# Retention and two MLPs on one core: scores of eight heads at once in block 1's chunks, key halves of heads 4 to 7 exchanged from chunk 0, block 1's norm by four small matmuls

## The chip, the cores and the metric

The kernel runs on one core of one Trainium2 chip. The core has TensorE (PE, with its weight loads listed as PEld), VectorE (DVE), ScalarE (ACT), GpSimd (POOL) and SyncE (SP), which here issues most DMAs. The metric is the device time of one launch in microseconds; lower is better.

## The reference

Three layers over 4 x 768 = 3072 tokens of 512 features, all in float32:

```
for t in range(S):                                   # retention, 8 heads of 64, state 64 x 64 per head
    state = gamma[h] * state + k[t] (outer) v[t]
    y[t]  = scale * q[t] @ state
x  = y as [3072, 512]
xn = x / sqrt(mean(x*x, -1) + 1e-6) * rms_g          # RMS norm
x  = (silu(xn @ w_gate) * (xn @ w_val)) @ w_out      # 512 -> 1536 -> 512
h  = x @ w_in                                        # 512 -> 1024
e  = exp(h - max(h));  solu = h * e / (sum(e) + 1e-9)
out = (solu - mean) / sqrt(var + 1e-6) * g_ln @ w_out2   # 1024 -> 512
```

## The kernel before, in words

The 3072 tokens are 6 blocks of 512, a block is 4 chunks of 128 tokens, and 6 chunks make one of the 4 batches. Retention is computed chunk by chunk: scores of keys against queries inside the chunk (a matmul), times a table of decays `mtab` that is zero above the diagonal (the mask, on DVE), times the values; to that the state `U` of the chunks before adds its part through `qd` (queries times `qtab`), and `kd` (keys times `ktab`) makes the state's update. `kd` and `qd` are products on POOL.

All large matmuls are done in three, as high and low halves of both operands (`mm3`, lines 719 to 721; each 128 x 128 weights and 512 columns). For block n the loop `bc_block` goes over 12 groups of the hidden features: gate into PSUM bank GB, value into VB, Silu on ACT (L764), product on DVE (L736), split into halves on ACT and DVE (L98, L99), and `cmm` sums the output into X0 to X3. `de_block` is the last MLP. Block 5 goes through `seven_block`, with 7 instead of 8 products per pair.

Weights come as packed 64-bit words. While block 0 runs, each of the 36 tiles of 512 KB is loaded (L595, a ring of four buffers `x`), turned into float32 (ACT L617, DVE L619, POOL L620; the sign on ACT into PSUM bank YB, L625; DVE L632 joins them), split into halves (ACT L98, DVE or POOL L99) and used; ACT's queue stores the halves to DRAM (`scr`) for later blocks. From the end of block 0 on the 16 tiles of the last MLP follow the same way (`w2i`, `w2o`).

Retention and norm of block n+1 are cut into pieces and laid in slots of block n (`extra`, `att_pieces`). Block 0's own chunks 0 to 3 stand at the start (`first_*`). A list scheduler with its own timeline then decides the order of the instructions on each engine; `run` (L117 issues its matmuls) keeps a group of matmuls together, and `issue_after` pins one instruction behind another.

There are two ways of doing a chunk before:

- Chunks 4 to 7 (block 1, while block 0 runs) go by units of 4 heads: `unit_load` (L137, L140, L143), `unit_prep` (L153, L161), `unit_scores` (L169: 4 matmuls of 64 rows x 128 keys x 128 queries into bank SB; mask L171) and `unit_out`.
- Chunks 8 to 23 go by all 8 heads: `att_load` (8 loads of 64 rows, L215, and 3 for keys and values), `att_prep` (L232, L237), `att_scores` (16 matmuls of 64 x 64 tiles of the array, a 64-key half each, without the half above the diagonal, into SB and YB; 6 masks L258, 4 memsets L260). Keys of heads 4 to 7 lie with their halves exchanged there, so `turn_tables` loads those halves of `mtab` and `ktab` the other way round between chunk 7 and chunk 8.

Block 1's norm has a path of its own: `rms_1` (four one-column matmuls L328, then L329 and L330 make `rinv`, the inverse root, one column per chunk), `rms_2` (L334: DVE lays `rinv` on a diagonal, 128 x 512; L337: one float32 matmul with ones spreads it over the partitions, into SB), `rms_mul` (four products L340), `xn_split` (halves `xnh`, `xnl`).

Of the kernel before, what the change touches and what calls it, by code (L numbers as in the profile page):

```python
# [9 lines left out]
F32 = mybir.dt.float32  # L10
# [30 lines left out]
def retention_moe_kernel(ctx: ExitStack, tc: tile.TileContext, qk0, q2, kt, kv, wpk, w2i, w2o,  # L41
# [92 lines left out]
    def unit_load(gc, u):  # L134
        gap("gq", 416)
        tq = wt("rq", [P, 4, P], F32, 2)
        nc.sync.dma_start(tq, q2[gc, u])  # L137
        if u == 0:
            rawk[gc] = wt("rk", [P, 4, P], F32, 2)
            nc.sync.dma_start(rawk[gc], kt[gc])  # L140
        gap("gr", 96)
        tv = wt("rv", [P, 512], F32, 2)
        nc.sync.dma_start(tv, kv[gc, u])  # L143
        raw[gc, u] = (tq, tv)

    def unit_prep(gc, u):
        tq, tv = raw.pop((gc, u))
        tk = rawk[gc] if u == 0 else rawk.pop(gc)
        kd = qd = None
        if gc % CPB != CPB - 1:  # L150
            gap("gd", 416)
            kd = wt("kd", [P, 4, 64], F32, 2)
            nc.gpsimd.tensor_tensor(  # L153
                out=kd, in0=tv[:, 0:256].rearrange("p (h d) -> p h d", h=4),
                in1=ktab_t[:, 4 * u:4 * u + 4].unsqueeze(2).to_broadcast([P, 4, 64]), op=ALU.mult)
        if gc % CPB != 0:
            qd = wt("qd", [P, 2, P], F32, 2)
            tq4 = tq.rearrange("p (a b) i -> p a b i", b=2)
            for hh in range(2):
                r = halfrows(hh)  # L160
                nc.gpsimd.tensor_tensor(out=qd[r], in0=tq4[r, :, hh, :],  # L161
                                        in1=qtab_t[r, 2 * u:2 * u + 2, :], op=ALU.mult)
        r = halfrows(u)
        prepd[gc, u] = (tk[r], tq[r], tv, kd, qd)

    def unit_scores(gc, u):
        tk, tq, tv, kd, qd = prepd[gc, u]
        for hl in range(4):
            nc.tensor.matmul(SB[:, hl * P:hl * P + P], lhsT=tk[:, hl, :], rhs=tq[:, hl, :], start=True, stop=True)  # L169
        A = masked[gc, u] = wt("r2", [P, 4, P], F32, 8)  # L170
        nc.vector.tensor_tensor(out=A, in0=SB.rearrange("p (h i) -> p h i", h=4),  # L171
                                in1=mtab_t[:, 4 * u:4 * u + 4, :], op=ALU.mult)

    def unit_out(gc, u):

        tk, tq, tv, kd, qd = prepd.pop((gc, u))
        A = masked.pop((gc, u))
        first, last = gc % CPB == 0, gc % CPB == CPB - 1
        ps = slice(2 * u, 2 * u + 2)
        calls = []  # L180
        if not first:
            calls += [mm(SB[:, pl * P:pl * P + P], U[gc % 2][:, 2 * u + pl, :], qd[:, pl, :], pl == 0, False)
                      for pl in range(2)]
        for pl in range(2):
            for hh in range(2):
                hl = 2 * pl + hh
                calls.append(mm(SB[halfrows(hh), pl * P:pl * P + P], tv[:, 256 + 64 * hl:320 + 64 * hl],
                                A[:, hl, :], first, first or pl == 1))
        sv = SB[:, 256:384].rearrange("p (a e) -> p a e", a=2)
        if not last:  # L190
            for pl in range(2):
                for hh in range(2):
                    hl = 2 * pl + hh
                    calls.append(mm(sv[halfrows(hh), pl, :], kd[:, hl, :], tv[:, 256 + 64 * hl:320 + 64 * hl],
                                    True, True))
        run(calls)
        if not last:
            for hh in range(2):
                decay_add(gc, halfrows(hh), ps, sv[halfrows(hh)])
        c = gc % NCB  # L200
        cs = slice(c * P, c * P + P)
        nc.scalar.copy(xT[:, ps, cs], SB[:, 0:256].rearrange("p (a i) -> p a i", a=2))
        if u:
            sq = f4()[:, 0, :].rearrange("p (a i) -> p a i", a=4)
            nc.scalar.activation(sq, xT[:, :, cs], AF.Square)
            nc.vector.tensor_reduce(out=ssq[:, cs], in_=sq.rearrange("p a i -> p i a"), axis=AX.X, op=ALU.add)

    def att_load(gc):
        tq, tk = wt("rq", [P, 4, P], F32, 2), wt("rk", [P, 4, P], F32, 2)
        tv = wt("rv", [P, 2, 512], F32, 2)  # L210
# [5 lines left out]
        nc.sync.dma_start(tv[:, 0], kv[gc, 0])  # L216
        for r in range(2):
            nc.sync.dma_start(tv[halfrows(r), 1], kv[gc, 1, halfrows(1 - r)])
        raw[gc] = (tq, tk, tv)

    def turn_tables():

        for r in range(2):
            nc.sync.dma_start(mtab_t[halfrows(r), 4:8, :], mtab[halfrows(1 - r), 4:8, :])
            nc.sync.dma_start(ktab_t[halfrows(r), 4:8], ktab[halfrows(1 - r), 4:8])

    def att_prep(gc):
        tq, tk, tv = raw.pop(gc)
        kd = qd = None
        if gc % CPB != CPB - 1:  # L230
            kd = wt("kd", [P, 2, 4, 64], F32, 2)
# [99 lines left out]

    def rms_2(bank):

        nc.vector.tensor_tensor(out=ssq.rearrange("p (c i) -> p c i", c=NCB),  # L334
                                in0=ident.unsqueeze(1).to_broadcast([P, NCB, P]),
                                in1=rinv.unsqueeze(2).to_broadcast([P, NCB, P]), op=ALU.mult)
        nc.tensor.matmul(bank, lhsT=ones, rhs=ssq, start=True, stop=True)  # L337

    def rms_mul(bank, k):
        nc.vector.scalar_tensor_tensor(out=xT[:, k, :], in0=xT[:, k, :], scalar=rg_t[:, k:k + 1], in1=bank,  # L340
# [159 lines left out]
    def att_pieces(n):  # L500

        out = []
        if n == 1:
            units = [(gc, u) for gc in range(NCB, 2 * NCB) for u in range(2)]
            ahead = units + [(2 * NCB,), (2 * NCB + 1,)]
            for i, (gc, u) in enumerate(units):
                nxt, nx2 = ahead[i + 1], ahead[i + 2]

                def a(gc=gc, u=u, nxt=nxt):
                    unit_scores(gc, u)  # L510
                    if len(nxt) == 1:
                        turn_tables()

                def b(nxt=nxt):
                    (unit_prep if len(nxt) == 2 else att_prep)(*nxt)

                def c(gc=gc, u=u, nx2=nx2):
                    unit_out(gc, u)
                    (unit_load if len(nx2) == 2 else att_load)(*nx2)

                out += [a, b, c]
# [321 lines left out]
    def seven_2(j, part, y, q):  # L843
# [5 lines left out]
        room[2] += 1  # L849
        V = nc.vector  # L850
        V.tensor_tensor(out=y[:, 0, hi], in0=d, in1=q[:, lo], op=ALU.add)
        V.tensor_tensor(out=y[:, 1, lo], in0=c, in1=q[:, lo], op=ALU.add)

    def seven_block(n):
        base = n * NM
        for j in range(NM // 2):
# [19 lines left out]
            nc.scalar.activation(gf[:, 256:], gf[:, 256:], AF.Silu)  # L876
            if j and not final:
                out(m - 1)
            seven_2(j, 1, *v)
# [1 line left out]
            nc.vector.tensor_tensor(out=vf[:, lo], in0=quads[1][0], in1=gf[:, lo], op=ALU.mult)  # L881
            nc.vector.tensor_tensor(out=vf[:, hi], in0=vf[:, hi], in1=gf[:, hi], op=ALU.mult)
            if final and PRE & 2:
                nc.scalar.activation(wt("sm", [P, 12], F32, 4)[:, 0:1], gf[:, 0:1], AF.Exp)
            for i in range(2):
                if i:
                    nc.vector.tensor_tensor(out=vf[:, 512:], in0=vf[:, 512:], in1=gf[:, 512:], op=ALU.mult)
# [352 lines left out]
```

## Time and profile before

| | |
|---|---|
| median of 3 runs | 993.0 us (991.95 to 993.1) |
| profiled execution | 992.89 us, its span 991.1 us, so 1.8 us lie around the span |
| mean granted TensorE clock | 0.995 |
| PE busy | 975.8 us of the span |
| DVE, ACT, POOL busy | 466.0, 398.0, 422.9 us |
| DMA | 211.90 MB, 214 GB/s on average |

A busy share over the whole span is an average of stages: chunks 0 to 3 (about 35 us), block 0 with its weight conversions (to about 159 us), and the rest. In a row of the timeline, "x8" joins eight records of one kind; the profile writes two records for each float32 matmul of the scores. "[1.50 <-ACT xT L202]" means that the engine stood idle for 1.50 us until the named instruction ended.

### The profile page before, as it was taken

The page shows a single profiled execution, that of the slowest core. Times are in us where ns is not written, and L with a number is a line of the kernel's source. Part 1 is how long each engine was busy: PE and PEld are TensorE (multiplying, and loading weights), DVE is VectorE, ACT ScalarE, POOL GpSimd, SP SyncE. Part 2 cuts the span into 40 slices and gives each one's busy share as a digit, 9 for nine tenths or more (in the row PEclk, how much of TensorE's full clock was granted, in tenths as well). Part 3 has the DMA queues.
Part 4 walks back from the last instruction along what each step waited for, and adds up shares of the span by engine and source line. Part 5 has one row for each costly group of instructions (what it writes and reads, how often), then busy time and mean ns, then how long its engine had stood idle before and what let it go on. Part 6 is the DMA issues. An engine that isn't in the chain of part 4 may idle for free.

```text
span 991.1 us, 15941 instructions
## 1 busy us (share of the span) xinstructions
PE 975.8 (98%) x5910; PEld 811.3 (82%) x5910; DVE 466.0 (47%) x921; ACT 398.0 (40%) x770; POOL 422.9 (43%) x517
## 2 busy tenths in 40 slices
PE   8899999999999999999999999999999999999998
PEld 8778787787888887888888888788888888999887
DVE  5788784563364743234462224462323353443552
ACT  4767664573344443222443122344212344221433
POOL 6876873672142593243644223644042382000031
PEclk9899999999999999999999999999999999999999
DMA  9699999796612135799522889622597724697200
GB/s 353 230 327 406 356 309 382 275 340 214 213 38 76 54 105 188 278 301 302 187 75 97 287 284 304 221 71 100 170 347 268 264 84 149 205 308 263 75 12 32
DMA packets 91021, 211.90 MB, mean 214 GB/s; under 512 B 10432, under 2 KB 36416, under 8 KB 90944
## 3 DMA queue, kind: packets, MB, share of 16 engines
q1 hardware_dynamic: 82160, 185.71, 55.3%
q10 hardware_dynamic: 8784, 25.17, 6.5%
q8 instruction: 47, 0.77, 0.3%
q14 instruction: 30, 0.25, 0.1%
HBM read 172.05 MB, written 38.80 MB: 213 GB/s over the span
## 4 chain that ended last, share of the span: by engine, by line
PE 86%; POOL 4%; DVE 3%; DMA 2%; ACT 2%; issue 2%; SPq 0%; ACTq 0%; POOLq 0%; DVEq 0%
PE X L719 12%; PE X L720 11%; PE X L721 11%; PE GB L719 7%; PE GB L721 7%; PE GB L720 6%; PE VB L719 6%; PE VB L720 6%; PE VB L721 6%; PE SB L117 3%; PE YB L117 2%; PE VB L825 2%; PE YB L825 2%; POOL st L620 1%; PE SB L825 1%
## 5 line engine op out<-in xcount | busy, mean ns | idle before, releaser
L736 DVE TENSOR_TENSOR f<-VB,f 128x512 f32<-128x512 f32 x60 | 41.3, 689 | 159.2 <-PE VB L721 151.4
L719 PE MATMUL X<-r,wo 128*128 128x512 f32 x264 | 101.7, 396 | 2.1 <-ACT r L98 1.5
L720 PE MATMUL X<-r,wo 128*128 128x512 f32 x264 | 103.4, 392 | 0.0
L721 PE MATMUL X<-r,wo 128*128 128x512 f32 x264 | 103.0, 390 | 0.0
L764 ACT ACTIVATE f<-GB 128x512 f32<-128x512 f32 x60 | 35.6, 594 | 147.6 <-PE GB L721 145.3
L98 ACT CAST r<-f 128x512 fp32r<-128x512 f32 x72 | 44.5, 619 | 120.8 <-DVE f L736 101.3
L620 POOL TENSOR_TENSOR st<-st,x 128x512 int32<-128x512 int32 x52 | 71.4, 1377 | 50.4 <-ACT st L994 11.6
L719 PE MATMUL GB<-xnh,w 128*128 128x512 f32 (+1 forms) x220 | 86.7, 394 | 2.7 <-ACT xnh L98 1.3
L719 PE MATMUL VB<-xnh,w 128*128 128x512 f32 (+1 forms) x220 | 85.8, 390 | 0.0
L720 PE MATMUL GB<-xnl,w 128*128 128x512 f32 (+1 forms) x220 | 85.6, 389 | 0.1
L721 PE MATMUL VB<-xnh,w 128*128 128x512 f32 (+1 forms) x220 | 85.2, 387 | 0.3 <-POOL w L99 0.3
L721 PE MATMUL GB<-xnh,w 128*128 128x512 f32 (+1 forms) x220 | 85.5, 388 | 0.0
L720 PE MATMUL VB<-xnl,w 128*128 128x512 f32 (+1 forms) x220 | 85.2, 387 | 0.0
L99 DVE TENSOR_TENSOR r<-f,r 128x512 fp32r<-128x512 f32 x72 | 61.9, 861 | 30.7 <-ACT r L98 30.2
L560 POOL TENSOR_TENSOR x<-x 128x512 f32<-128x512 f32 x24 | 30.8, 1288 | 105.2 <-DMA x<-scr 83.1
L950 POOL TENSOR_TENSOR sm<-sm 128x1 f32<-128x1 f32 x24 | 5.3, 222 | 138.3 <-DVE sm L928 121.0
L719 PEld LDWEIGHTS X<-r,wo 128*128 128x128 f32 x264 | 49.4, 188 | 13.3 <-ACT r L98 2.1
L721 PEld LDWEIGHTS X<-r,wo 128*128 128x128 f32 x264 | 49.6, 188 | 10.3
L720 PEld LDWEIGHTS X<-r,wo 128*128 128x128 f32 x264 | 49.6, 188 | 10.2 <-DVE r L99 0.2
L719 PE MATMUL X<-w2oh,r 128*128 128x512 f32 (+1 forms) x144 | 56.6, 393 | 0.0
L721 PE MATMUL X<-w2oh,r 128*128 128x512 f32 (+1 forms) x144 | 55.7, 387 | 0.0
L720 PE MATMUL X<-w2ol,r 128*128 128x512 f32 (+1 forms) x144 | 55.3, 384 | 0.0
(370 smaller groups left out, 2420.1 us busy)
## 6 DMA issues: line engine op xcount, KB each, us to landing
w<-scr SPq DMA_DIRECT2D x96, 512.0 KB, 4.6
wo<-scr SPq DMA_DIRECT2D x60, 512.0 KB, 4.4
x<-in_wpk SPq DMA_DIRECT2D x36, 512.0 KB, 6.6
x<-scr SPq DMA_DIRECT2D x24, 512.0 KB, 6.7
sscr<-x SPq DMA_DIRECT2D x24, 512.0 KB, 7.7
scr<-CV ACTq DMA_DIRECT2D x18, 512.0 KB, 6.5
rv<-in_kv SPq DMA_DIRECT2D x24, 256.0 KB, 4.6
scr<-w ACTq DMA_DIRECT2D x12, 512.0 KB, 6.0
```

What stands on the lines that cost most here:

```text
L98: h = nc.scalar.copy(hi, src)
L99: (lo_eng or nc.vector).tensor_tensor(out=lo, in0=src, in1=hi.bitcast(F32), op=ALU.subtract)
L117: return lambda: nc.tensor.matmul(out, lhsT=lhsT, rhs=rhs, start=start, stop=stop)
L560: nc.gpsimd.tensor_tensor(out=w[:, 0, :], in0=w[:, 0, :], in1=w[:, 1, :], op=ALU.add)
L620: nc.gpsimd.tensor_tensor(out=ti, in0=ti, in1=lo, op=ALU.add)
L719: nc.tensor.matmul(ps, lhsT=lh, rhs=rh, start=start, stop=False)
L720: nc.tensor.matmul(ps, lhsT=lh, rhs=rl, start=False, stop=False)
L721: nc.tensor.matmul(ps, lhsT=ll, rhs=rh, start=False, stop=stop)
L736: recent["dve"] = nc.vector.tensor_tensor(out=a, in0=GV[1], in1=silu[:, 0, :], op=ALU.mult)
L764: recent["act"] = nc.scalar.activation(s[:, 0, :], GV[0], AF.Silu)
L825: nc.tensor.matmul(ps, lhsT=x, rhs=y[:, k, :], start=start and k + i == 0, stop=k == 1 and i == 2, skip_group_check=True)
L950: G.tensor_tensor(out=w, in0=r, in1=r, op=ALU.mult)
```

## The change

Chunks 4 to 7 use `att_load`, `att_prep` and `att_scores`, as chunks 8 to 23 do, and a new `half_out` for the output of four heads at a time. The score banks are SB and YB, so YB alternates between the masks and the signs of the weight conversion. The key halves of heads 4 to 7 are exchanged from chunk 0: the tables are loaded so at the start, `kv_load` replaces one load by three in chunks 0 to 3, `first_scores` becomes 16 matmuls per chunk, and `turn_tables` is gone. Block 1's `rms_2` becomes four matmuls that take a broadcast column of `rinv` as weights and the identity as data, with no work on DVE. In block 5 one sum for the second half moves behind the first half's products, and the load of the Exp table is pinned behind the last Silu.

```
-    def unit_scores(gc, u):
-        tk, tq, tv, kd, qd = prepd[gc, u]
-        for hl in range(4):
-            nc.tensor.matmul(SB[:, hl * P:hl * P + P], lhsT=tk[:, hl, :], rhs=tq[:, hl, :], start=True, stop=True)
-        A = masked[gc, u] = wt("r2", [P, 4, P], F32, 8)
-        nc.vector.tensor_tensor(out=A, in0=SB.rearrange("p (h i) -> p h i", h=4),
-                                in1=mtab_t[:, 4 * u:4 * u + 4, :], op=ALU.mult)
...
+    def half_out(gc, u):
+        tq, tk, tv, kd, qd = prepd[gc] if u == 0 else prepd.pop(gc)
+        A = [masked[gc, hh] if u == 0 else masked.pop((gc, hh)) for hh in range(2)]
...
+    def kv_load(t, gc):
+        nc.sync.dma_start(t[:, 0], kv[gc, 0])
+        for r in range(2):
+            nc.sync.dma_start(t[halfrows(r), 1], kv[gc, 1, halfrows(1 - r)])
...
     def rms_2(bank):
-        nc.vector.tensor_tensor(out=ssq.rearrange("p (c i) -> p c i", c=NCB),
-                                in0=ident.unsqueeze(1).to_broadcast([P, NCB, P]),
-                                in1=rinv.unsqueeze(2).to_broadcast([P, NCB, P]), op=ALU.mult)
-        nc.tensor.matmul(bank, lhsT=ones, rhs=ssq, start=True, stop=True)
+        for c in range(NCB):
+            nc.tensor.matmul(bank[:, c * P:c * P + P], lhsT=rinv[:, c:c + 1].to_broadcast([P, P]), rhs=ident,
+                             start=True, stop=True)
...
     def first_load(c):
         nc.sync.dma_start(QK[:, c], qk0[c])
-        nc.sync.dma_start(KV[:, c], kv[c].rearrange("u p x -> p u x"))
+        kv_load(KV[:, c], c)
     def first_scores(c, banks):
-        run([mm(banks[hh][:, p * P:p * P + P], QK[halfrows(hh), c, 1, p, :], QK[halfrows(hh), c, 0, p, :], True, True)
-             for p in range(4) for hh in range(2)])
+        run([mm(banks[hh][halfrows(half), p * P:p * P + P],
+                QK[halfrows(hh), c, 1, p, halfrows(half if p < 2 else 1 - half)], QK[halfrows(hh), c, 0, p, :], True, True)
+             for p in range(4) for hh, half in ((0, 0), (1, 1), (0, 1), (1, 0))])
...
+            for gc in range(NCB, 2 * NCB):
+                out += [lambda gc=gc: att_scores(gc), lambda gc=gc: att_prep(gc + 1), lambda gc=gc: half_out(gc, 0),
+                        lambda gc=gc: (half_out(gc, 1), att_load(gc + 2))]
...
     def seven_2(j, part, y, q):
...
-        V.tensor_tensor(out=y[:, 1, lo], in0=c, in1=q[:, lo], op=ALU.add)
+        if part == 0:
+            V.tensor_tensor(out=y[:, 1, lo], in0=c, in1=q[:, lo], op=ALU.add)
...
     nc.sync.dma_start(QK[:, 0], qk0[0])
-    nc.sync.dma_start(mtab_t, mtab)
-    nc.sync.dma_start(ktab_t, ktab)
+    for t, src in ((mtab_t, mtab), (ktab_t, ktab)):
+        nc.sync.dma_start(t[:, 0:4], src[:, 0:4])
+        for r in range(2):
+            nc.sync.dma_start(t[halfrows(r), 4:8], src[halfrows(1 - r), 4:8])
     nc.sync.dma_start(utab_t, utab)
-    nc.sync.dma_start(KV[:, 0], kv[0].rearrange("u p x -> p u x"))
+    kv_load(KV[:, 0], 0)
...
-    unit_load(NCB, 0)
-    unit_load(NCB, 1)
-    unit_prep(NCB, 0)
+    att_load(NCB)
+    att_load(NCB + 1)
+    att_prep(NCB)
```

What this does to the order on TensorE, at the scores of one chunk among the matmuls of block 0. Before, one unit of four heads (lines 719 to 721 are the large matmuls, `CV` and `w` weights):

```order
216 L719 MATMUL GB<-xnh,CV 128x512
217 L720 MATMUL GB<-xnl,CV 128x512
218 L169 MATMUL SB<-rq_630,rk_632 128x128 x4
219 L721 MATMUL GB<-xnh,CV 128x512
220 L719 MATMUL GB<-xnh,CV 128x512
```

And of the changed kernel the group of eight heads (left out are three more pairs of each shape), whose large matmuls are lines 666 to 668:

```order
307 L668 MATMUL GB<-xnh,w_85_845 128x512
308 L117 MATMUL YB<-rq_567,rk_568 64x128
309 L117 MATMUL SB<-rq_567,rk_568 64x128
...
316 L117 MATMUL YB<-rq_567,rk_568 64x64
317 L117 MATMUL SB<-rq_567,rk_568 64x64
...
324 L666 MATMUL GB<-xnh,w_85_845 128x512
325 L667 MATMUL GB<-xnl,w_85_845 128x512
```

Two groups of four full-width matmuls per chunk have become one group of sixteen, eight of 64x128 and eight of 64x64, in turns into YB and SB.

The second place is TensorE at the end of block 0, around the matmul that spreads `rinv`. Before (`xnh` with `CV` is still block 0's last value group, with `w_202` it is block 1's first gate):

```order
554 L720 MATMUL VB<-xnl,CV 128x512
555 L337 MATMUL SB<-ssq,ones 128x512
556 L721 MATMUL VB<-xnh,CV 128x512
557 L719 MATMUL VB<-xnh,CV 128x512
558 L720 MATMUL VB<-xnl,CV 128x512
559 L721 MATMUL VB<-xnh,CV 128x512
560 L721 MATMUL X_70<-r_200_1575,wo_1425 128x512
561 L720 MATMUL X_71<-r_201_1576,wo_1425 128x512
562 L721 MATMUL X_71<-r_200_1575,wo_1425 128x512
563 L719 MATMUL GB<-xnh,w_202_1593 128x512
```

And now (`w_188` is block 1's first gate tile):

```order
676 L668 MATMUL X_69<-r_192_1739,CV 128x512
677 L667 MATMUL X_70<-r_193_1740,CV 128x512
678 L668 MATMUL X_70<-r_192_1739,CV 128x512
679 L667 MATMUL X_71<-r_193_1740,CV 128x512
680 L668 MATMUL X_71<-r_192_1739,CV 128x512
681 L297 MATMUL SB<-ident,rinv 128x128 x4
682 L666 MATMUL GB<-xnh,w_188_1698 128x512
683 L666 MATMUL VB<-xnh,w_190_1718 128x512
```

Seven matmuls of block 0 stood between the spreading matmul and block 1's first; now none does, and all of block 0's stand ahead of it.

The third place is SP's queue of loads at the start. Before, to the third-last of the rows that the chunks' loads and the first weight tiles share:

```order
19 L595 DMA x_31_438<-in_wpk 128x512
20 L137 DMA rq_508<-in_q 128x512
21 L140 DMA rk_510<-in_kt 128x512
22 L143 DMA rv_513<-in_kv 128x512
23 L137 DMA rq_515<-in_q 128x512
24 L143 DMA rv_517<-in_kv 128x512
25 L140 DMA rk_632<-in_kt 128x512
26 L595 DMA x_34_450<-in_wpk 128x512
27 L595 DMA x_37_462<-in_wpk 128x512
28 L595 DMA x_40_474<-in_wpk 128x512
```

And now (L184 are the loads of 64 rows):

```order
26 L184 DMA rk_553<-in_kt 64x2x128 x4
27 L184 DMA rq_552<-in_q 64x2x128
28 L542 DMA x_34_494<-in_wpk 128x512
29 L184 DMA rq_552<-in_q 64x2x128 x3
30 L171 DMA rv_555<-in_kv 128x512
31 L173 DMA rv_555<-in_kv 64x512
32 L542 DMA x_37_506<-in_wpk 128x512
33 L173 DMA rv_555<-in_kv 64x512
34 L184 DMA rk_568<-in_kt 64x2x128 x3
35 L542 DMA x_40_518<-in_wpk 128x512
```

The weight tile `x_40` had 27 loads ahead of it (each row's "x" counted); now it has 47, nearly all of the new ones of 64 rows.

## Rows read from the trace of the kernel before

**Rows 1.** The page: busy time of TensorE; the chain that ended last.

```profile
PE 975.8 (98%) x5910; PEld 811.3 (82%) x5910; DVE 466.0 (47%) x921; ACT 398.0 (40%) x770; POOL 422.9 (43%) x517
...
PE 86%; POOL 4%; DVE 3%; DMA 2%; ACT 2%; issue 2%; SPq 0%; ACTq 0%; POOLq 0%; DVEq 0%
```

**Rows 2.** Waits of TensorE: line, releaser, us in total, times, longest.

```profile
PE X L719 <- ACT r L98: 1.5, 1, 1.5
PE SB L169 <- ACT xT L202: 1.5, 1, 1.5
...
PE GB L719 <- ACT xnh L98: 1.3, 1, 1.3
...
PE VB L721 <- POOL w L99: 0.3, 1, 0.3
```

**Rows 3.** Timeline of TensorE around one unit's scores: start, us, operation.

```profile
80.12 0.39 PE L720 MATMUL VB<-xnl,w 128*128 128x512 f32 x1
80.44 1.16 PE L169 MATMUL SB<-rq,rk 64*128 64x128 f32 x8
...
81.87 0.39 PE L719 MATMUL VB<-xnh,w 128*128 128x512 f32 x1
```

**Rows 4.** The same around the eight heads' scores of a later chunk.

```profile
265.76 0.39 PE L719 MATMUL X<-r,wo 128*128 128x512 f32 x1
...
266.22 0.39 PE L721 MATMUL X<-r,wo 128*128 128x512 f32 x1
266.54 0.32 PE L117 MATMUL YB<-rq,rk 64*64 64x128 f32 x1
...
267.70 0.39 PE L720 MATMUL GB<-w2il,x 128*128 128x512 f32 x1
```

**Rows 5.** Masks on DVE, by line: count, ns min/median/max, first and last.

```profile
L171 DVE TENSOR_TENSOR r<-SB,mtab_t x8: 678/686/693, 39.3 to 135.0; 128x512 f32<-128x512 f32 x8
...
L258 DVE TENSOR_TENSOR A<-YB,mtab_t x48: 270/294/426, 243.6 to 765.1; 64x128 f32<-64x128 f32 x32, 128x256 f32<-128x256 f32 x16
```

**Rows 6.** The products kd and qd on POOL, by line.

```profile
L153 POOL TENSOR_TENSOR kd<-rv,ktab_t x6: 612/1001/1069, 35.0 to 126.6; 128x256 f32<-128x256 f32 x6
...
L161 POOL TENSOR_TENSOR qd<-rq,qtab_t x12: 719/734/1175, 35.6 to 119.6; 64x256 f32<-64x256 f32 x12
...
L232 POOL TENSOR_TENSOR kd<-rv,ktab_t x13: 1033/1045/1489, 140.9 to 651.2; 128x512 f32<-128x512 f32 x13
...
L237 POOL TENSOR_TENSOR qd<-rq,qtab_t x14: 1272/1287/1722, 133.6 to 691.0; 128x512 f32<-128x512 f32 x14
```

**Rows 7.** The chain that ended last, at the start and at 39 us.

```profile
2.58 0.43 SPq L1042
3.06 5.87 DMA QK<-in_qk
...
38.95 0.69 POOL qd L161
```

**Rows 8.** Timeline of all engines where block 1 begins.

```profile
154.72 1.02 PE L337 MATMUL SB<-ssq,ones 128*128 128x512 f32 x2
...
155.78 2.72 DVE L340 SCALAR_TENSOR_TENSOR xT<-xT,rg_t,SB 128x512 f32<-128x512 f32 x4 [4.21 <-PE SB L337]
...
157.99 2.18 ACT L98 CAST xnh<-xT 128x512 fp32r<-128x512 f32 x4 [3.50 <-DVE xT L340]
...
158.66 0.49 PE L719 MATMUL GB<-xnh,w 128*128 128x512 f32 x1 [1.29 <-ACT xnh L98]
```

**Rows 9.** Windows of 25 us: busy us per engine, clock, DMA share, GB/s.

```profile
25.00:50.00 25.00, 22.24 (x153) 19.62 (x153) 19.02 (x30) 17.98 (x34) 22.60 (x25) 0.86 0.68 231
...
75.00:100.00 25.00, 25.00 (x123) 20.04 (x121) 20.47 (x29) 17.68 (x32) 16.89 (x15) 1.00 1.03 411
```

**Rows 10.** Waits of ACT up to 180 us, for the weight tiles' loads.

```profile
ACT x L617 <- DMA x<-in_wpk: 5.7, 5, 1.8
```

**Rows 11.** SP's issues of 64-row loads of a later chunk.

```profile
109.57 1.85 SPq L215 DMA_DIRECT2D rk<-in_kt  x3
```

More of the change, by code (lines that the diff above doesn't have):

```diff
@@ L132, in decay_add @@
             nc.vector.tensor_tensor(out=new, in0=new, in1=sv, op=ALU.add)
[L134 to L164, printed above, removed]
@@ L166, in unit_scores @@
-    def unit_scores(gc, u):
-        tk, tq, tv, kd, qd = prepd[gc, u]
-        for hl in range(4):
-            nc.tensor.matmul(SB[:, hl * P:hl * P + P], lhsT=tk[:, hl, :], rhs=tq[:, hl, :], start=True, stop=True)
-        A = masked[gc, u] = wt("r2", [P, 4, P], F32, 8)
-        nc.vector.tensor_tensor(out=A, in0=SB.rearrange("p (h i) -> p h i", h=4),
-                                in1=mtab_t[:, 4 * u:4 * u + 4, :], op=ALU.mult)
-    def unit_out(gc, u):
-        tk, tq, tv, kd, qd = prepd.pop((gc, u))
-        A = masked.pop((gc, u))
+    def half_out(gc, u):
+        tq, tk, tv, kd, qd = prepd[gc] if u == 0 else prepd.pop(gc)
+        A = [masked[gc, hh] if u == 0 else masked.pop((gc, hh)) for hh in range(2)]
@@ L178, in unit_out, with v @@
         first, last = gc % CPB == 0, gc % CPB == CPB - 1
         ps = slice(2 * u, 2 * u + 2)
+        def v(hl):
+            return tv[:, u, 256 + 64 * hl:320 + 64 * hl]
         calls = []
         if not first:
-            calls += [mm(SB[:, pl * P:pl * P + P], U[gc % 2][:, 2 * u + pl, :], qd[:, pl, :], pl == 0, False)
+            calls += [mm(SB[:, pl * P:pl * P + P], U[gc % 2][:, 2 * u + pl, :], qd[:, 2 * u + pl, :], pl == 0, False)
                       for pl in range(2)]
@@ L185, in unit_out @@
             for hh in range(2):
-                hl = 2 * pl + hh
-                calls.append(mm(SB[halfrows(hh), pl * P:pl * P + P], tv[:, 256 + 64 * hl:320 + 64 * hl],
-                                A[:, hl, :], first, first or pl == 1))
+                calls.append(mm(SB[halfrows(hh), pl * P:pl * P + P], v(2 * pl + hh),
+                                A[hh][:, 2 * u + pl, :], first, first or pl == 1))
         sv = SB[:, 256:384].rearrange("p (a e) -> p a e", a=2)
@@ L193, in unit_out @@
                     hl = 2 * pl + hh
-                    calls.append(mm(sv[halfrows(hh), pl, :], kd[:, hl, :], tv[:, 256 + 64 * hl:320 + 64 * hl],
-                                    True, True))
+                    calls.append(mm(sv[halfrows(hh), pl, :], kd[:, u, hl, :], v(hl), True, True))
         run(calls)
@@ L206, in unit_out @@
             nc.vector.tensor_reduce(out=ssq[:, cs], in_=sq.rearrange("p a i -> p i a"), axis=AX.X, op=ALU.add)
+    def kv_load(t, gc):
+        nc.sync.dma_start(t[:, 0], kv[gc, 0])
+        for r in range(2):
+            nc.sync.dma_start(t[halfrows(r), 1], kv[gc, 1, halfrows(1 - r)])
     def att_load(gc):
+        gap("gq", 416)
         tq, tk = wt("rq", [P, 4, P], F32, 2), wt("rk", [P, 4, P], F32, 2)
+        gap("gr", 96)
         tv = wt("rv", [P, 2, 512], F32, 2)
@@ L215, in att_load @@
                     nc.sync.dma_start(t[halfrows(hh), 2 * u:2 * u + 2, :], heads[:, :, hh, :])
-        nc.sync.dma_start(tv[:, 0], kv[gc, 0])
-        for r in range(2):
-            nc.sync.dma_start(tv[halfrows(r), 1], kv[gc, 1, halfrows(1 - r)])
+        kv_load(tv, gc)
         raw[gc] = (tq, tk, tv)
[L221 to L225, printed above, removed]
     def att_prep(gc):
@@ L230, in att_prep @@
         if gc % CPB != CPB - 1:
+            gap("gd", 416)
             kd = wt("kd", [P, 2, 4, 64], F32, 2)
@@ L503, in att_pieces @@
         if n == 1:
[L504 to L521, printed above, removed]
+            for gc in range(NCB, 2 * NCB):
+                out += [lambda gc=gc: att_scores(gc), lambda gc=gc: att_prep(gc + 1), lambda gc=gc: half_out(gc, 0),
+                        lambda gc=gc: (half_out(gc, 1), att_load(gc + 2))]
             return out
@@ L875, in seven_block @@
             gf, vf = (x.rearrange("p a i -> p (a i)") for x in (g, v[0]))
-            nc.scalar.activation(gf[:, 256:], gf[:, 256:], AF.Silu)
+            silu = nc.scalar.activation(gf[:, 256:], gf[:, 256:], AF.Silu)
             if j and not final:
@@ L883, in seven_block @@
             if final and PRE & 2:
-                nc.scalar.activation(wt("sm", [P, 12], F32, 4)[:, 0:1], gf[:, 0:1], AF.Exp)
+                with tc.issue_after(silu.ins):
+                    nc.scalar.activation(wt("sm", [P, 12], F32, 4)[:, 0:1], gf[:, 0:1], AF.Exp)
             for i in range(2):
                 if i:
+                    nc.vector.tensor_tensor(out=v[0][:, 1, lo], in0=quads[1][2], in1=v[1][:, lo], op=ALU.add)
                     nc.vector.tensor_tensor(out=vf[:, 512:], in0=vf[:, 512:], in1=gf[:, 512:], op=ALU.mult)
```

## Prediction

> **What bounds the kernel now.** I read the page first. TensorE is busy 98% of the span, and the chain that ended last is 86% TensorE, the next engine 4% [rows 1]. So a microsecond taken from TensorE's stream is a microsecond of the time, as long as nothing that feeds it comes late; and what another engine saves is worth nothing except where TensorE waits for it. Second I read what TensorE waits for: the waits named there are single ones of 1.5 us and less [rows 2]. The work to judge is therefore (a) TensorE's own time in the replaced matmuls, (b) those few waits, (c) whether the new order makes feeders late. For (a) the busy column is no good, since records overlap; I read the timeline and take the time between the starts of the large matmuls on both sides of the group.
>
> **Scores of chunks 4 to 7: -6.2 us.** Large matmuls follow each other every (266.22 - 265.76) / 2 = 0.23 us [rows 4], which I call a step. Around one unit's scores, from the matmul at 80.12 to the second one behind the group at 81.87, there are 1.75 us [rows 3]; two steps are 0.46, so a unit of four heads costs 1.29 us. Eight units: 10.3 us. Around the eight heads' group of a later chunk the same reading is 267.70 - 266.22 = 1.48 us [rows 4], less 0.46 gives 1.02 us. It is the same code that chunks 4 to 7 now run, so four groups cost 4.1 us. The difference is 6.2 us. The output matmuls keep count and shape: two halves of four heads per chunk. Bounds: from 0 (the new group costs as much as two units) to -10.3 (the whole of the old ones).
>
> **The masks and POOL's products: 0.** DVE's masks go from two of 0.686 us to six of about 0.29 (four) and 0.43 (two), that is from 1.37 to about 2.0 us per chunk [rows 5]. Both lie beside TensorE's other work: DVE is busy 20.5 of 25 us in the window at 75 us [rows 9], so there are some 4 us of room for 0.65. What is queued behind the masks on DVE is the joining of a weight tile, and YB is now shared: ACT's next sign waits until the masks have read YB, and they wait for the scores. I give this no price of its own but put it in the term for late weights below. On POOL a chunk's kd and qd were 2 x 1.0 + 4 x 0.73 = 4.9 us and become 1.05 + 1.29 = 2.3 [rows 6]. Four memsets of the masks come to it, each with a quarter of kd's columns, so by an estimate from kd's row a quarter of its 1.05 us, together 1.0: some 1.6 us less per chunk. POOL is 16.9 of 25 us busy there [rows 9], off the path, and worth nothing in that stretch. In the first chunk of these it is on it: at 39 us the chain runs through POOL's qd [rows 7]. The gain there is between 0 and 1.6 us, once; it goes into the next term.
>
> **The start and the weight tiles: +1.0 us, between -1.6 and +9.4.** The first chunk's queries are on the path: the chain goes from SP's issue to the landing of QK at 8.93 us [rows 7]. That load is issued first still, but tables and values follow in 12 issues up to the second QK where there were 6, and one issue takes about 0.47 us (2.58 to 3.06 from one start to the next) [rows 7]; so the second chunk's loads go out some 2.8 us later. The chunks behind the first run one after another through POOL and ACT, and part of that time is regained because fewer products stand on POOL. Next, the weight tile `x_40` has 47 issues ahead of it instead of 27. If issue alone set the time, that would be 20 x 0.47 = 9.4 us; the three 64-row issues that the trace shows went out at 1.85 us for three [rows 11], slower still. But issue is not all that sets it: the DMA engines are only 68% busy from 25 to 50 us [rows 9], and there SP spends most of its time waiting for buffers, not issuing. Bytes go down, not up: 1.05 MB per chunk (8 x 64 KB + 3 loads of 512 KB in all) against 1.31 MB (5 of 256 KB), since each query is loaded once. I take +1.0: nearer to the small end, as ACT's waits for weight tiles are 5.7 us in five waits [rows 10], of which only one or two reached TensorE.
>
> **Waits that go: -1.6 us.** TensorE waits 1.5 us for ACT's copy xT before a unit's scores, 0.3 for a weight's low half on POOL, and 1.5 for r before an output matmul [rows 2]. The first arises since SB was still to be read by ACT, which stood behind a late tile; in the new order there are half as many groups of scores into SB, at other places. The last stands in block 1's first groups, whose order now differs. Of the sum of 3.3 us I count one half; bounds 0 and -3.3. Late next would be the same feeders in other places, which is the term above.
>
> **Where block 1 begins: +1.6 us.** Before, the spreading matmul L337 is followed by seven matmuls of block 0; L340 starts at 155.78, xnh at 157.99, and block 1's first matmul at 158.66, after an idle time of 1.29 us [rows 8]. The chain from the spread (end at 155.74) to that first matmul is 2.9 us; the seven steps hid 1.6 of them. In the new order nothing is left to stand between, so the whole 2.9 us are idle: +1.6 us. The four small matmuls (4 x 128 columns of float32) have the same number of columns as the one of 512 that they replace (1.02 us) [rows 8]: 0. The DVE product that goes (L334) was hidden by block 0's matmuls, and so is its absence: 0. Bounds: 0 if the list order lets block 0's last matmuls run late enough to cover the chain anyway, +3.3 if xnl and a late value tile also wait.
>
> **The tail: 0.** In block 5 TensorE's first wait is a DMA of the output weights; one DVE sum moves later, to just ahead of its use, and the load of the Exp table keeps to ACT's idle time. I cost both at nothing: TensorE's matmuls of the first half hide them. Without that cover it is one sum of 256 columns, half of the 0.69 us that DVE takes for 512 [rows 5].
>
> **Sum.** -6.2 + 1.0 - 1.6 + 1.6 + 0 = -5.2 us. The profiled execution took 992.89 us (span 991.1 and 1.8 around it), 0.1 below the median of 993.0: 992.9 - 5.2 = 987.7 us. Its own range: 984 to 990.5.
>
> **Rivals.**
>
> *Half of the gain is lost to late weights.* In the window from 75 to 100 us the DMA engines are full (1.03) [rows 9]. With eight loads of 64 rows per chunk taking the queue's places, tiles come later, and their conversion waits once more for YB. If each of four chunks makes TensorE wait 0.7 us, +2.8 beyond the forecast: 990.5. For it speaks the full DMA; against it that of all TensorE's waits only the one of 0.3 us names a weight [rows 2], so some lead exists.
>
> *Slower: the loads at the start set the pace of block 0.* Place: the first groups of block 0 behind the start, where the weight wait of 0.3 and the wait for xT behind a late tile show that tiles come just in time [rows 2]. If SP's issues are the limit, `x_40` comes 9.4 us later and TensorE waits as long: 992.9 - 6.2 - 1.6 + 1.6 + 9.4 = 996.1. It decides from about 8.2 us of delay on: there the sum is 2 us above before. For it: one issue after another is on the chain at the start [rows 7]. Against: the DMA share of 0.68 [rows 9], which means that SP waits rather than works. The Trainium skill, DMA: Bandwidth & Descriptors, Rules for kernel authors, speaks against this part of the change: it says that two transfers to disjoint halves of the partitions share the same engines, so that one of 128 partitions should be used. By that rule alone the split loads would gain nothing and the issues be pure cost, the 996.1 above; the rows bear it out only as far as the 1.85 us for three issues, as no load of both kinds stands side by side.
>
> *The change does not do what it says: the exchange does not pay.* If a group of sixteen 64 x 64 tiles costs among block 0's matmuls what two units cost (2.6 us), the scores give 0, and 992.9 + 1.0 - 1.6 + 1.6 = 993.9, less what the waits give: within 0.2% of before. Against it stands the reading of 1.03 us, taken between the same kind of large matmuls [rows 4].
>
> **How the numbers follow.** About 0.2% (2 us) is what a measurement of this kernel can tell from no change. Chances: the forecast 0.60, half lost 0.18, slower start 0.11, no pay 0.05, and 0.06 for more than forecast (all waits gone, POOL's gain at the start, no cost where block 1 begins: 992.9 - 6.2 - 1.6 - 3.3 + 0 = 981.8). Faster by over 2 us is all of the forecast, over half of the second case and the last: 0.60 + 0.10 + 0.06 = 0.76. Within: 0.08 + 0.05 = 0.13. Slower: 0.11. The range that leaves out two in ten: 982 to 993.5.
>
> **What would show it.** Right: around each of four groups 1.0 to 1.1 us between large matmuls less two steps, where eight of 1.3 were; the first gate matmul of block 0 within 2 us of where it starts before; an idle time of 2.5 to 3.3 us in front of block 1's first matmul; a span of block 0 from its first gate matmul to block 1's shorter by about 5. Wrong: waits of TensorE on weights' halves in block 0 that sum to over 3 us, or a first gate matmul over 3 us later. If the four groups measure over 2 us each, the first term was wrong; if the whole is under 983, the waits and the start gave more than I count.

## The result: 1.4% slower, and the profile after

The changed kernel took 1007.57 us (median of 4 runs, 1007.18 to 1010.26) against 993.05 us before in the same job: ratio 1.0139, 95% interval 1.0117 to 1.0161. The forecast was 987.7 us, the range 982.0 to 993.5: wrong in sign, by 20 us. The profiled execution took 1007.34 us, its span 1005.6 us. Two executions that took far longer, one of the kernel before (1383.47 us) and one of experiment 7 (4250.32 us), are left out of all ratios.

The page of the changed kernel, rows answering to [rows 1] (busy us and share; then the chain that ended last by engine):

```profile
PE 975.2 (97%) x6044; PEld 811.5 (81%) x6044; DVE 464.3 (46%) x936; ACT 396.6 (39%) x768; POOL 420.4 (42%) x521
...
PE 82%; DMA 7%; DVE 3%; POOL 3%; ACT 2%; issue 1%; SPq 1%; ACTq 0%; POOLq 0%; DVEq 0%
```

TensorE's busy time is the same within a microsecond, DMA went from 2% to 7% of the chain: the time came in as waiting. What TensorE waits for in the changed kernel, answering to [rows 2]:

```profile
PE GB L666 <- ACT f L711: 6.1, 4, 4.2
PE X L666 <- ACT r L98: 4.7, 1, 4.7
PE X L317 <- ACT f L308: 4.5, 2, 4.0
...
PE GB L666 <- ACT xnh L98: 1.5, 1, 1.5
...
PE GB L667 <- DVE xnl L99: 1.2, 1, 1.2
```

Three single waits of 4.0 to 4.7 us, all for ACT, where the longest was 1.5. To see where the time went in, I counted the large matmuls of both traces (all that come in three, two of 256 columns as one of 512; the gated MLP of a block holds 432 of them) and took the time at which the n-th starts, in us:

| n | before | changed | difference |
|---|---|---|---|
| first | 35.4 | 41.9 | +6.5 |
| 180 | 90.4 | 93.8 | +3.4 |
| 240 | 107.6 | 115.8 | +8.2 |
| 400 | 151.5 | 158.2 | +6.7 |
| 456 (block 1's first groups) | 167.4 | 183.8 | +16.4 |
| 2000 | 566.1 | 580.5 | +14.4 |

So three places: the start (+6.5), the stretch around 100 us (+4.8), and the passage from block 0 to block 1 (+9.7). Between them the change gives time back (-3.1, -1.5, -2.0). The n-th matmul is not always the same one in both orders, so the rows between the first and the last are good to a microsecond or two.

**The scores do what was forecast.** TensorE around the second chunk's group of the changed kernel (start, us, operation):

```profile
82.65 0.39 PE L668 MATMUL GB<-xnh,w 128*128 128x512 f32 x1
82.97 0.32 PE L117 MATMUL YB<-rq,rk 64*64 64x128 f32 x1
...
84.13 0.39 PE L667 MATMUL GB<-xnl,w 128*128 128x512 f32 x1
```

84.13 - 82.65 = 1.48 us, as in [rows 4], so 1.02 us per group where two units cost 2.58 [rows 3]. All three groups that lie among large matmuls (the first chunk's stands in the start) read the same.

**The start.** SP's issues, the changed kernel first, then the one row of before that answers to the first weight tile:

```profile
1.17 0.42 SPq L990 DMA_DIRECT2D mtab_t<-in_mtab  x1
1.64 1.20 SPq L992 DMA_DIRECT2D mtab_t<-in_mtab  x2
...
10.77 0.43 SPq L171 DMA_DIRECT2D KV<-in_kv  x1
11.90 1.96 SPq L173 DMA_DIRECT2D KV<-in_kv  x2
13.90 0.58 SPq L542 DMA_DIRECT2D x<-in_wpk  x1
...
23.80 2.73 SPq L184 DMA_DIRECT2D rk<-in_kt  x4
```

```profile
6.52 0.47 SPq L595 DMA_DIRECT2D x<-in_wpk  x1
```

Ten more issues of 0.4 to 0.6 us each stand ahead of the first weight tile, and SP stands still twice among them, for 0.7 us (11.20 to 11.90) and for 1.0 us (inside the 1.96), until an earlier transfer has landed; so the tile goes out 7.4 us later. The transfers themselves are slower too. From 10 to 20 us (columns as in [rows 9]; the kernel before, then the changed one):

```profile
10.00:20.00 10.00, 10.00 (x141) 9.10 (x140) 6.25 (x12) 4.61 (x12) 8.38 (x10) 0.88 1.03 398
```

```profile
10.00:20.00 10.00, 8.46 (x117) 7.27 (x118) 2.89 (x6) 2.14 (x6) 5.21 (x7) 0.68 1.05 299
```

The DMA engines are full in both (1.03 and 1.05), but with the split loads they move 299 GB/s and not 398. What the late tile does is seen on ACT, which takes its instructions in order (changed kernel; in brackets the idle time and what ended it):

```profile
20.80 0.80 ACT L564 ACTIVATE x<-x,two 128x512 f32<-128x512 uint32 x1 [3.17 <-DMA x<-in_wpk]
...
26.01 0.77 ACT L564 ACTIVATE x<-x,two 128x512 f32<-128x512 uint32 x1 [2.10 <-DMA x<-in_wpk]
...
27.75 0.59 ACT L308 ACTIVATE f<-SB 128x512 f32<-128x512 f32 x1
```

L308 is the square for the norm of the second chunk. It has nothing to do with weights, but the scheduler put the conversions of two tiles ahead of it, and those wait for late loads. TensorE's 4.0 us for L308 are that.

**Around 100 us.** TensorE waits 4.2 us for a Silu (L711), whose input was complete when its last gate matmul, started at 94.72, had ended. ACT's idle times ahead of it, then TensorE (changed kernel):

```profile
95.32 0.76 ACT L564 ACTIVATE x<-x,two 128x512 f32<-128x512 uint32 x1 [0.97 <-DMA x<-in_wpk]
...
99.37 0.62 ACT L98 CAST w<-st 128x512 fp32r<-128x512 f32 x1 [2.24 <-DVE st L579]
...
101.17 0.76 ACT L564 ACTIVATE x<-x,two 128x512 f32<-128x512 uint32 x1 [0.66 <-DMA x<-in_wpk]
...
102.84 0.62 ACT L98 CAST wo<-st 128x512 fp32r<-128x512 f32 x1 [0.66 <-DVE st L579]
...
104.45 0.58 ACT L711 ACTIVATE f<-GB 128x512 f32<-128x512 f32 x1
```

```profile
105.08 0.50 PE L666 MATMUL GB<-xnh,w 128*128 128x512 f32 x1 [4.16 <-ACT f L711]
```

The Silu stands behind the conversions of several weight tiles, and these wait for late loads and for DVE, which joins their parts.

**From block 0 to block 1.** ACT of the changed kernel, with the DMA issues in its queue (ACTq), and then the row of the chain that ended last which explains it:

```profile
159.43 0.36 ACTq L612 DMA_DIRECT2D scr<-CV  x1
159.89 0.37 ACT L164 COPY xT<-SB 128x256 f32<-128x256 f32 x1 [3.46 <-DMA x<-in_w2i]
160.29 0.63 ACT L167 ACTIVATE f<-xT 128x512 f32<-128x512 f32 x1
166.80 0.33 ACTq L615 DMA_DIRECT2D scr<-CV  x1
167.17 0.60 ACT L711 ACTIVATE f<-GB 128x512 f32<-128x512 f32 x1 [6.25 <-DMA x<-in_w2i]
```

```profile
153.62 13.10 DMA x<-in_w2i
```

L711 is the Silu of block 0's last group; its input was long there. In front of it in ACT's queue stands a store (L615), and the store was issued only when a load that has nothing to do with it, issued at 153.62, had landed at 166.72. The program's waits say why: its DMAs, loads of SP and stores of ACT alike, take eight semaphores in turn, and each waits until the one eight places before it, on the same semaphore, has landed. (DMAHW5_49 is the name of one of the eight. In the trace the 644 DMAs use eight semaphores, 80 or 81 on each, and this store and this load the same one.)

```
ACT  197 L615 DMA scr_2_122<-CV 128x1024 [waits DMAHW5_49,Pool_49]
SP   131 L542 DMA x_207_1838<-in_w2i 128x512 [waits DMAHW5_49,Activation_49,Pool_49]
```

So a store in ACT's queue holds all of ACT until a load is in. The kernel before has this too, at the same seam:

```profile
157.62 0.33 ACTq L668 DMA_DIRECT2D scr<-CV  x1
```

That store went out when a load issued at 147.77 had landed at 157.54, and the cast of `xnh` behind it came at 157.99 [rows 8], though L340's four products start at 155.78 and take 0.7 us each. TensorE after the hold in the changed kernel:

```profile
169.51 2.07 PE L666 MATMUL X<-r,CV 128*128 128x512 f32 x4 [4.67 <-ACT r L98]
171.38 0.63 PE L667 MATMUL X<-r,CV 128*128 128x512 f32 x1
171.81 0.63 PE L668 MATMUL X<-r,CV 128*128 128x512 f32 x1
...
174.42 1.05 PE L297 MATMUL SB<-ident,rinv 128*128 128x128 f32 x8
176.96 0.50 PE L666 MATMUL GB<-xnh,w 128*128 128x512 f32 x1 [1.49 <-ACT xnh L98]
...
178.89 0.50 PE L667 MATMUL GB<-xnl,w 128*128 128x512 f32 x1 [1.19 <-DVE xnl L99]
```

After 4.67 us of idleness the matmuls follow each other at 0.43 us and not at 0.23: the granted clock is half, 1.2 GHz and not 2.4 (0.50 from 168 to 173 us). Some ten steps of that are another 2 us. Then comes the norm with nothing of block 0 left to stand between: 1.49 and 1.19 us. The windows of the changed kernel (columns as in [rows 9]) show the mean clock around each of the three places. The kernel before has 0.86 in the first window as well [rows 9], and 1.00 in the other two:

```profile
25.00:50.00 25.00, 18.93 (x176) 16.90 (x177) 17.75 (x29) 17.70 (x38) 19.67 (x19) 0.86 0.96 297
100.00:125.00 25.00, 20.84 (x124) 16.38 (x123) 18.64 (x31) 16.14 (x29) 16.20 (x18) 0.93 0.87 314
150.00:175.00 25.00, 19.81 (x98) 15.67 (x97) 9.70 (x17) 11.33 (x21) 12.22 (x12) 0.86 1.01 364
```

### The profile page after: what moved, and what is told of

It is laid out like the page before. It is cut to its first block, busy times and chain, and to the rows that moved or that the text cites. A ratio compares the mean times of both kernels' runs of the same rounds, so it can differ in the third digit from the quotient of the medians.

```text
span 1005.6 us, 16289 instructions
## 1 busy us (share of the span) xinstructions
PE 975.2 (97%) x6044; PEld 811.5 (81%) x6044; DVE 464.3 (46%) x936; ACT 396.6 (39%) x768; POOL 420.4 (42%) x521
## 3 DMA queue, kind: packets, MB, share of 16 engines
q1 hardware_dynamic: 85232, 184.40, 55.7%
## 4 chain that ended last, share of the span: by engine, by line
PE 82%; DMA 7%; DVE 3%; POOL 3%; ACT 2%; issue 1%; SPq 1%; ACTq 0%; POOLq 0%; DVEq 0%
PE X L666 11%; PE X L668 11%; PE X L667 11%; PE GB L666 7%; PE GB L668 6%; PE GB L667 6%; PE VB L666 6%; PE VB L668 6%; PE VB L667 6%; DMA x<-in_wpk 3%; PE SB L117 3%; PE YB L117 2%; PE VB L772 2%; PE YB L772 2%; DMA x<-in_w2i 1%
## 5 line engine op out<-in xcount | busy, mean ns | idle before, releaser
L711 ACT ACTIVATE f<-GB 128x512 f32<-128x512 f32 x60 | 35.8, 596 | 154.3 <-PE GB L668 148.0
L99 DVE TENSOR_TENSOR r<-f,r 128x512 fp32r<-128x512 f32 x72 | 59.5, 827 | 32.5 <-ACT r L98 31.8
L666 PEld LDWEIGHTS GB<-xnh,w 128*128 128x128 f32 x220 | 41.7, 190 | 16.9 <-ACT f L711 5.9
```

Of the source, the lines that this page charges most:

```text
L99: (lo_eng or nc.vector).tensor_tensor(out=lo, in0=src, in1=hi.bitcast(F32), op=ALU.subtract)
L666: nc.tensor.matmul(ps, lhsT=lh, rhs=rh, start=start, stop=False)
L711: recent["act"] = nc.scalar.activation(s[:, 0, :], GV[0], AF.Silu)
```

## Experiments

All ratios are to the kernel before in the same job, with the 95% interval; differences between versions are good to 1.5 to 3 us. One thing limits all of them: after an edit the list scheduler orders the instructions anew. Of the versions here only whole_oldrms keeps the order of ACT's instructions of the version that it starts from. So part of any other difference can be a new order.

**1. One load each (whole_all).** The host lays the arrays out in the order of the tiles; before it was 11 loads for a chunk, now 3, and the start has 10 issues fewer.

```
+    qa, ka = pairrows(qT), pairrows(kT)
+    kvt = np.stack([kv[:, 0], np.roll(kv[:, 1], 64, axis=1)], axis=2)
...
-                    nc.sync.dma_start(t[halfrows(hh), 2 * u:2 * u + 2, :], heads[:, :, hh, :])
-        kv_load(tv, gc)
+        nc.sync.dma_start(tk, ka[gc])
+        nc.sync.dma_start(tq, qa[gc])
+        nc.sync.dma_start(tv, kvt[gc])
```

> The changed kernel with every split load made one: the arrays lie in DRAM already in the order of the tiles, so tables and chunks 0 to 3 need one load each again, and each of chunks 4 to 23 needs 3 loads instead of 11. Theory I (SP's queue of issues is what came late): the first gate matmul of block 0 returns to 35 to 37 us, the wait of 4.2 us at 100 us goes, and the time falls to 986 to 993 us. Theory II (the common bank YB and the new order of the conversions cost the time, whatever the loads): the first gate matmul stays behind 40 us or the waits at 100 and 164 us stay, and the time is 1000 us or more.

Measured: 994.83 us, ratio 1.0005 (0.9993 to 1.0018); first gate matmul at 33.7 us. 12.7 us of the loss are gone with the splits; the time is 2 us above theory I's range, and the wait of 4.2 us has become one of 1.9. By the count of large matmuls it leads before by 2.5 us at n = 400 and trails by 2.3 at n = 2000: the loss at block 1's beginning remains, which theory I did not cover. The edit changes more than the number of issues: the rows that the host lays out are longer, and the loads' queue has 63,792 packets in place of 85,232 for the same 184.4 MB.

**2. Only the start whole (start_whole); 3. only the chunks from 4 on whole (att_whole).** Each takes one half of the edit above.

> The changed kernel with only the tables and the values of chunks 0 to 3 loaded whole; chunks 4 to 23 keep their 11 loads. Theory I: the 10 issues saved ahead of the first weight tile bring the first gate matmul to 37 us or earlier and take 6 to 9 us off: 998 to 1002 us, while the waits at 100 and 164 us stay. Theory II: no more than 2 us off, 1005 to 1008 us.

> The changed kernel with chunks 4 to 23 loaded by 3 loads each; tables and chunks 0 to 3 keep their split loads. Theory I: the start stays late (first gate matmul at 40 to 42 us), tiles of the later groups come in time, so the wait at 100 us goes: 996 to 1002 us. Theory II: the waits stay, 1005 us or more.

Measured: 1010.93 us, ratio 1.0176 (1.0158 to 1.0194), and 1005.58 us, ratio 1.0121 (1.0091 to 1.0152). Both miss theory I's numbers, and the second falls into theory II's range. In the second the first gate matmul comes at 38.7 us and a wait of 2.3 us at 103 us stays. With the start whole the kernel is no faster than with all loads split. The first gate matmul comes at 41.2 us there although the first weight tile is issued at 6.62. Its ACT shows what takes the place (rows of the version with only the start whole, and then one of its SP):

```profile
25.18 0.60 ACT L98 CAST w<-st 128x512 fp32r<-128x512 f32 x1
31.47 0.37 ACTq L612 DMA_DIRECT2D scr<-w  x1
31.89 0.60 ACT L308 ACTIVATE f<-YB 128x512 f32<-128x512 f32 x1 [6.11 <-DMA rk<-in_kt]
```

```profile
27.66 1.18 SPq L184 DMA_DIRECT2D rk<-in_kt  x2
```

A store held ACT for 6.11 us behind one of the 64-row loads of chunk 5's keys, which come earlier in this version; that load went out only at 27.66, when ACT had stood still for 1.9 us, and landed at 31.39. So it is not the count of issues alone: it is also where a store falls among them. That made a theory S, tested in 6.

**4. The kernel before with its start's loads split (before_split).**

```
-    nc.sync.dma_start(mtab_t, mtab)
+        nc.sync.dma_start(t[:, 0:4], src[:, 0:4])
+        for r in range(2):
+            nc.sync.dma_start(t[halfrows(r), 4:8], src[halfrows(r), 4:8])
```

> The kernel before with one thing added: tables and values of chunks 0 to 3 loaded in the same pieces as in the changed kernel (10 more issues ahead of the first weight tile, same bytes, same places, nothing exchanged). Theory I: the first gate matmul comes 4 to 7 us later and the time is 997 to 1000 us. Theory II (the number of issues costs nothing as long as the bytes are the same): 993 us within 1 us.

Measured: 998.65 us, ratio 1.0052 (1.0035 to 1.0069); first gate matmul at 41.7 us (35.4 before), nearly the 41.9 of the changed kernel. Splitting the start's loads alone, with the same bytes to the same places, costs 6.3 us at the start and 5 us in the end: theory I's numbers. That the number of issues does it all is not shown, for two more things come with the split. From 10 to 20 us the full DMA engines move 333 GB/s and not 398 (this version):

```profile
10.00:20.00 10.00, 7.83 (x92) 7.06 (x93) 4.69 (x10) 3.03 (x8) 7.63 (x10) 0.83 1.04 333
```

And TensorE, after an idle time of 2.63 us at 28.26, has a granted clock of 0.50 from 30 to 41 us, where before it was 1.00 up to 32.8. So part of the 6.3 us is the half clock.

**5. The place of the norm (whole_span26) and its form (whole_oldrms),** both on the version with whole loads.

```
-                begin, span, r = 0, 30, (31, 32, 33, 33, 33, 33, 34, 34, 35, 35)
+                begin, span, r = 0, 26, (31, 32, 33, 33, 33, 33, 34, 34, 35, 35)
```

> The version with whole loads (994.8 us), with the 16 pieces of block 1's retention laid over slots 0 to 26 of block 0 instead of 0 to 30, so that the norm's four matmuls stand ahead of block 0's last group and not behind it. Theory P (the place of the norm behind all of block 0 costs the time there, idle TensorE first, half clock after it): the waits for xnh and xnl (1.5 and 1.2 us) and the half clock behind them go, 988 to 991 us. Theory F (the new form of the norm is what costs): 993 us or more.

> The version with whole loads, with only block 1's norm done as before (product on DVE, one matmul with ones). Its place in TensorE's order stays behind all of block 0. Theory P: the same waits as with the new form, 994 to 997 us. Theory F: 988 to 991 us.

(The second puts the product L334 and the one matmul with ones back.) Measured: 989.41 us, ratio 0.9944 (0.9927 to 0.9961), and 996.41 us, ratio 1.0016 (1.0000 to 1.0031). The place decides, as theory P has it: with the pieces over 26 slots the norm's matmuls stand in the last group of block 0 and block 1's first gate matmul waits for nothing (the version with 26 slots):

```profile
149.88 0.39 PE L664 MATMUL GB<-xnl,CV 128*128 128x512 f32 x1
150.11 1.05 PE L294 MATMUL SB<-ident,rinv 128*128 128x128 f32 x8
150.92 0.48 PE L665 MATMUL GB<-xnh,CV 128*128 128x512 f32 x1
```

The old form at the late place is no better; whether it is worse by a microsecond, the intervals do not tell.

**6. The stores on SP's queue (after_sp),** the changed kernel otherwise untouched.

```
         with tc.issue_after(h.ins):
-                nc.scalar.dma_start(*stores.pop())
+                nc.sync.dma_start(*stores.pop())
```

> The changed kernel with one edit: the stores of the converted halves are issued from SP's queue instead of ACT's. Theory S (ACT stands behind a store whose place in the ring of eight transfers is still taken by a load, and everything behind it on ACT waits): TensorE's waits for ACT at 100 us and at 164 us (4.2 and 4.7 us) shrink below 2 us each, 997 to 1003 us, while the late start stays. Theory T (the weight tiles themselves come late, whoever issues the stores): the waits stay in some form, 1005 us or more.

Measured: 998.37 us, ratio 1.0044 (1.0023 to 1.0065), 9.2 us below the changed kernel though all its loads stay split. The wait of 4.7 us for r is gone from the list, and the one for the Silu at 100 us is down to 0.8; a new one of 2.2 us stands at 130 us (changed kernel with stores on SP):

```profile
PE GB L666 <- ACT f L711: 3.7, 4, 2.2
PE X L317 <- ACT f L308: 3.5, 1, 3.5
...
PE GB L666 <- ACT xnh L98: 1.5, 1, 1.5
PE GB L667 <- DVE xnl L99: 1.2, 1, 1.2
```

The waits of the start and of the late norm stay, as they should. Theory S holds for the wait of 4.7 us, in front of which the trace shows the store. For the one at 100 us it is not shown: no store stands in ACT's idle times there, and the wait is gone as well in the version of experiment 8 that has 26 slots and leaves its stores on ACT. There it is the conversions that come late, and what shortened it in both versions was not separated.

**7. The signs in SBUF (whole_sq),** on the version with whole loads: `g = wt("sq", [P, 512], F32, 1)` for all tiles.

> The version with whole loads, with the signs of all tiles written to a buffer in SBUF instead of the bank YB, so that scores and signs share no bank. If the shared bank holds conversions up (theory II), the waits on tiles in block 0 (1.9 us at 94 us, 1.3 at 64, 1.1 at 57) shrink and the time falls by 2 us or more, to 990 to 993 us. If it does not, 994 us within 1 us.

Measured: 1005.64 us (1004.54 to 1006.38 without the execution left out), ratio 1.0104 (1.0072 to 1.0137). Neither outcome: slower by some 10 us. Probably the one buffer in SBUF holds things up itself: TensorE waits 3.8 us in three for tiles on POOL, 2.5 for DVE's product and 3.9 for masks, where with whole loads it waited 1.3 for a tile on POOL and for none of the others. What the common bank costs is not settled by it. ACT waits 6.9 us in three for masks before it writes a sign into YB in the changed kernel, and 4.3 with whole loads; whether any of that reaches TensorE was not separated.

**8. All together (whole_26_sp), the two edits that touch no load (after_span26, after_26_sp), and a control (before_sp).**

> Whole loads, pieces over 26 slots, and the stores on SP's queue. The three causes add if they are separate: the wait of TensorE for ACT of 2.7 us at 115 us in the version without the last edit goes with the half clock behind it, 984 to 988 us. If the store's place on ACT costs nothing where loads are few, 989 us within 1.5 us.

> The changed kernel with only the pieces laid over slots 0 to 26. Theory P: the norm's chain is covered, so 4 to 9 us of the loss at the end of block 0 goes: 998 to 1003 us. If the loads decide there too (the store behind a load holds ACT wherever the norm stands), 1005 us or more.

> The changed kernel with both edits that touch no load: pieces over 26 slots and stores on SP. What is left against before should then be the late start (first gate matmul 5 to 6 us late) less the scores' gain: 992 to 996 us. If the two edits mend the same loss, 998 us as with the stores alone.

> The kernel before with only its stores moved to SP's queue: the control. Theory S says that the store on ACT costs because many small loads fill the ring of eight; before has few, so 992 to 994 us. If stores on ACT cost whatever the loads, 988 us or less.

| version | us | ratio (interval) |
|---|---|---|
| whole loads, 26 slots, stores on SP | 987.31 | 0.9928 (0.9913 to 0.9944) |
| changed, 26 slots | 996.60 | 1.0018 (1.0003 to 1.0034) |
| changed, 26 slots, stores on SP | 992.61 | 0.9987 (0.9974 to 1.0000) |
| before, stores on SP | 989.19 | 0.9950 (0.9933 to 0.9968) |

The first and the third have the times that the theories gave, and the second lies 1.4 us under its range. In the first the time is not the proof that it looks: the wait that was to go is still there, as 3.5 us at 115 us, with half a clock behind it (0.50 from 116.3 to 119.8 us), and 987.3 is also within 0.2 us of the other outcome, 989 within 1.5 (first version):

```profile
PE GB L663 <- ACT f L708: 6.2, 5, 3.5
```

The second took off 11 us, more than the waits of the norm themselves: with the norm earlier, the store's hold of ACT near 160 us shrinks to 1.9 us, since the store and the loads fall differently, and TensorE does not wait there. Apart the two scheduling edits take 9.2 and 11.0 us, together 15.0: they mend partly the same wait. The control missed: moving the stores takes 5.0 us (3.2 to 6.7) off the kernel before as well, where loads are few. So the hold is not made by the split loads; in its longest case they only lengthen it, as the store at 157.62 above shows. The first version beats both kernels; most of what it gains over before (6.9 us) is to be had from before by moving the stores alone (5.0 us).

## Why the prediction was wrong, step by step

- **What bounds the kernel: right.** TensorE still does, and feeders that come late are paid in full. I read too little from it: the change gave every engine a new order, and I looked for late feeders only in the loads and in TensorE's own list of waits.
- **Scores, -6.2 us: right** per group (1.02 us measured). Of the eight units one stood in the start and so did one of the four new groups, so among the large matmuls it is 7 x 1.29 - 3 x 1.02 = 6.0 us.
- **"The start and the weight tiles: +1.0 us": this step failed.** It measured +6.5 us at the first gate matmul and +4.8 us more between n = 180 and 240. I counted issues to the second QK and to `x_40` and put 9.4 us as the far end, but not those to the first weight tile (10 more, 7.4 us later). I took the DMA engines' idle share from 25 to 50 us for room that was needed before 25 us, where they are full (1.03 before, 1.05 now) and slower with split loads. I also misread a row: the load that lands at 8.93 us [rows 7] is the second chunk's QK, not the first's (which had landed at 4.2), and so it is not issued first; it went out 3.9 us later. And I looked for who waits for the tile only on TensorE (its wait for POOL's w), not on ACT, in whose queue the norm of chunks 1 to 3 stands behind the conversions.
- **"Where block 1 begins: +1.6 us": failed too.** It measured +9.7 us. The idle time that I forecast (2.5 to 3.3 us) came out as 1.49 + 1.19 = 2.7 us, but that is luck: it is two waits, for xnh and for xnl, and the chain from the spread to block 1's first matmul takes 1.5 us and not the 2.9 that I read from [rows 8]. Those 2.9 us held a store at 157.62, in front of the cast of `xnh`, and I read them as the chain. The same kind of store I did not see in the new order either: it held ACT behind a load of the last MLP's weights, which made the 4.67 us ahead of the norm, and the half clock behind that idle time made another 2. The order with its waits showed the store in front of the Silu; I read only the order.
- **Waits that go, -1.6 us:** the 1.5 us for xT and the 1.5 us for r before block 1's first output went (the new wait for r is another, at the end of block 0); larger ones came.
- **The rivals.** *Slower: the loads at the start set the pace of block 0* was the right place, with 996.1 us and a chance of 0.11, though not the whole loss. Experiment 4 gives the price of the split start alone: 5.0 us. It was argued away with a DMA share of 0.68 from a later window. The rule of the Trainium skill quoted there (DMA: Bandwidth & Descriptors, Rules for kernel authors: use one transfer of 128 partitions rather than two halves) fits what was measured: the same bytes in whole loads took 12.7 us off. As those loads also have longer rows, no run shows the price of the halves alone.
- **The tail, 0; masks, POOL's products, 0:** from n = 456 to 2000 the changed kernel gains 2.0 us, the wait of 1.5 us for r in block 1 among it; from there to the end it stays 14.3 to 14.5 us behind.

## What to carry to other kernels

Where loads are split, count the issues ahead of the first load that each stage waits for, in the queue that issues them, and compare what the full DMA engines move; the bytes alone do not tell. Then look on every in-order engine for what stands behind an instruction that waits for such a load, a store in a compute engine's queue above all. When pieces of work are moved, look at what is left to cover a serial chain at the seam between two stages.

## What the runs showed of the hardware that was not expected

The wait of a DMA issue for a place among eight transfers stops the compute engine in whose queue it stands: 6.11 us for one store at the start, 6.25 us for another. Full DMA engines moved 398 GB/s from 10 to 20 us with whole loads, 333 with the start's loads split and 299 in the changed kernel. After idle times of TensorE of 4.16 and 4.67 us, matmuls ran at 1.2 GHz: steps of 0.43 us in place of 0.23, some seven in the one case and ten in the other, so that the idle time of 4.67 us cost about 6.7.
